# Reading the state operands of a chunked attention readout from a copy that is ordered by chunks

## The chip, the cores and the metric

The kernel runs on one core of a Trainium2 chip. The metric is the device time of one execution in microseconds (us), median of several runs. TensorE (PE) multiplies matrices; a weight load (PEld) puts the stationary operand into the array, a matmul streams the moving operand past it. VectorE (DVE), ScalarE (ACT) and GpSimd (POOL) do the elementwise work, and SyncE (SP) issues most transfers.

## The reference

Three stages follow one another: a linear attention with a decay per key dimension, an MLP, and a mixture of experts with one expert per token.

```python
# attention: B=4, H=8, S=768, D=48
for t in range(S):
    state = alpha[:, :, t, :, None] * state + k[:, :, t, :, None] * v[:, :, t, None, :]
    y[:, :, t] = einsum('bhd,bhde->bhe', q[:, :, t], state)
# MLP over 3072 tokens of 384: h = x @ w_in (384x2048); x = (h - tanh(h)) @ w_out
# experts: e = argmax(x @ w_gate); out = gate * sigmoid * (relu(x @ w1[e]) @ w2[e])
```

## The kernel before

Tokens are worked off in 8 blocks of 384 (half a sequence of one batch entry). A **unit** is one block of one pair of heads, so a block has 4 units and there are 32. The two heads of a pair lie on partitions 0 to 47 and 64 to 111. Within a unit the 384 tokens are 6 chunks of 64.

For each unit: `prep_k` and `prep_q` scan the decays and scale keys and queries (DVE); `decay` writes the chunk decays into `GE` (ACT, L196); `turn_k` transposes the keys (PE, L226, copied out by ACT); `score` multiplies keys and queries within a chunk (PE, L242 and L243, stationary operand `kt`, 48 rows by 64 contiguous columns); `causal` masks the scores (DVE); `carry` and `update` put the state increments of the chunks into PSUM (L259, L268); `chain` runs one scan on DVE over them (L272) and writes the states ahead of every chunk to `SS[p]`, a tile of [128, 64, 7]: for each of 48 value dimensions (padded to 64) the 7 states stand next to each other, so that the 64 values of one chunk's state row are 7 elements apart. `readout` (L306) then adds, for each chunk, queries times state and scores times values: 12 matmuls with `SS` as the stationary operand and 12 with `WV`, whose 64 columns are contiguous, over the four 64x64 quarters of the array, into one PSUM pair. The trace shows each of these fp32 matmuls as two instruction pairs. ACT copies the result out (L309), `place` splits off its low part (DVE, L315) and SP moves it into the MLP's input `xT`.

The MLP of a block is 16 steps f: `h_step` (L409, 9 matmuls into `psh`, tanh on ACT L415, subtraction on DVE L419, cast to a high part on ACT L423, low part on DVE L424) and `x_step` (L434, 9 matmuls) of the step before. The units of the next block are woven into these steps, one unit per 4 steps: in phase 0 (f % 4) score, carry and update, in phase 1 chain, in phase 2 readout, in phase 3 turn_k.

Units 0 to 3 run ahead of block 0, in an order written out by hand. Units 4 to 7 run in block 0's steps (`first_block`), also in an order written by hand for PE, ACT, DVE and POOL, along with the conversion of the MLP's weights. From block 1 on the framework's scheduler orders PE, ACT, DVE and POOL by its own timeline model; SP's order is by hand until block 2. Units 8 to 31 run in blocks 1 to 6. Block 7 has no units, and the experts follow it (L936, L964, L870, L871, L982). Each engine takes its instructions in order.

Of the kernel before, what the change touches and what calls it, by code (L numbers as in the profile page):

```python
# [9 lines left out]
F32 = mybir.dt.float32  # L10
# [8 lines left out]
B, H, S, D = 4, 8, 768, 48  # L19
# [7 lines left out]
NC = TB // CH  # L27
NBLK = NT // TB
NP = H // 2
# [34 lines left out]
def tile_kernel(ctx, tc, aps, outs):  # L64
    nc = tc.nc
    pe, act, dve, pool, sp = nc.tensor, nc.scalar, nc.vector, nc.gpsimd, nc.sync
# [14 lines left out]
    ap1 = att.enter_context(tc.tile_pool(name="ap1", bufs=1, side="right"))  # L81
# [41 lines left out]
    X0 = [ap1.tile([128, TB], F32, name=f"X0{i}") for i in range(2)]  # L123
# [2 lines left out]
    WV = [ap1.tile([128, WW], F32, name=f"WV{i}") for i in range(2)]  # L126
    GE = [ap1.tile([128, D, NC + 1], F32, name=f"GE{i}") for i in range(2)]
    VZ = [ap1.tile([128, NA, 2, 2 * D], F32, name=f"VZ{i}") for i in range(2)]
    SS = [ap1.tile([128, 64, NC + 1], F32, name=f"SS{i}") for i in range(NP)]

    early = [(psx, "x0"), (psx, "x1"), (psx, "x2"), (psa, "at")] * 4
# [6 lines left out]
    def pair(name):  # L138
        return psy.tile([128, 2, 512], F32, tag="py", name=name)

    units = [(j, p) for j in range(NBLK) for p in range(NP)]
# [18 lines left out]
    def vz(u):  # L160
        return vzx[u] if u in vzx else VZ[u % 2]

# [89 lines left out]
    def carry(u):  # L252
# [5 lines left out]
        else:  # L258
            act.copy(pu[:, 0:n * D:n], SS[p][:, 0:D, NC])  # L259

# [10 lines left out]
    def chain(u):  # L271
        yield dve.tensor_tensor_scan(  # L272
            out=SS[units[u][1]][:, 0:D].rearrange("p d c -> p (d c)"), data0=GE[u % 2].rearrange("p d c -> p (d c)"),
            data1=st[u].pop("pu")[:, 0:(NC + 1) * D], initial=0.0, op0=ALU.mult, op1=ALU.add)

    def weave(*gens):
        gens = [iter(g) for g in gens]
        while gens:
            for g in list(gens):
                if next(g, gens) is gens:  # L280
                    gens.remove(g)
# [3 lines left out]
    def readout(u):  # L285
        j, p = units[u]
        s = st[u]
        ps = s.pop("py") if u >= NP else pair("psy")
        SP, h = SS[p], NC // 2

        for c in range(h):
            for x in range(2):
                for q in range(2):
                    for hh in range(2):
                        cc = q * h + c
                        cs = slice(cc * CH, (cc + 1) * CH)
                        o = ps[64 * q:64 * q + 64, hh, c * CH:(c + 1) * CH]
                        if x == 0:  # L300
                            rs = slice(64 * hh, 64 * hh + D)
                            w, m = SP[rs, :, cc], X0[u % 2][rs, cs]
                        else:
                            rs = slice(64 * hh, 64 * hh + CH)
                            w, m = WV[u % 2][rs, cc * D:cc * D + 64], X1[rs, cs]
                        pe.matmul(o, w, m, start=(c + x == 0), stop=(x == 1), skip_group_check=True)  # L306
        s["y"] = y = (g3.tile([128, 2, TB], F32R, tag="gg", name="y") if 0 < u < 4 else ap1.tile([128, 2, TB], F32R, tag="y", name="y"))
        s["py"] = ps
        act.copy(y[:, 0].rearrange("p (b t) -> p b t", b=2), ps[:, :, 0:TB // 2])  # L309
# [80 lines left out]
    def gate(f):  # L390
        wT, pl = gated.pop(f)
        for k in range(KC):
            pe.matmul(pl, wT[:, k], wg[:, k], start=(k == 0), stop=(k == KC - 1), skip_group_check=True)  # L393
        act.copy(WR[f][:, DM:DG], pl)

    def conv_next():
        nonlocal nconv
        nconv += 1
        return conv(nconv - 1)
# [75 lines left out]
    rs = {}  # L475
# [198 lines left out]
    for i in range(2):  # L674
        pool.memset(VZ[i][64:128, :, 0], 0.0)
        pool.memset(VZ[i][0:64, :, 1], 0.0)
        pool.memset(WV[i][:, NC * D:WW], 0.0)
    for p in range(NP):
        pool.memset(SS[p][:, D:64], 0.0)
    warm = psh.tile([128, 512], F32, tag="h", name="warm")  # L680
    junk = ones1[:, 0:192].bitcast(BF16)

# [13 lines left out]
    def K(u):  # L696
        weave(prep_k(u))
        turn_k(u)
# [63 lines left out]
    def first_block(f, pend):  # L762
        u, ph = NP + (f + 1) // 4, f % 4
        new = [conv_next()] if nconv < NF else []

        def head():

            gate(f)
            if ph == 0:
                if f:  # L770
                    decay(u)
                carry(u)
                score(u)
                update(u)
            elif ph == 1:
                if u > NP:
                    alpha_low(u)
            elif ph == 2:
                readout(u)
            act.copy(OH[:, f], WR[f])  # L780
            if f + 1 < NF:
                low_in(f + 1)
            for g in new:
                for _ in range(4 if wide else 0):
                    next(g)

        def middle():
            weave(*new)
            if pend and ph != 3:
                x_step(*pend)  # L790
            if ph == 0:
                weave(chain(u))
            elif ph == 1:
                weave(causal(u))
                weave(prep_k(u + 1))
            elif ph == 3:
                x_step(*pend)
                turn_k(u)
                weave(prep_q1(u))
                weave(prep_q2(u))  # L800

        gg = h_step(0, f, (head,))
        middle()
        if f >= NF - 2:
            low_out(f - NF + 2)
        if ph == 0:
            load_v(u + 2)
        elif ph == 1:
            if u > NP:
                load_unit(u + 2)  # L810
        elif ph == 2:
            place(u)
            load_w_v(u + 2)
        if f + 1 < NF:
            gate_turn(f + 1)
        if ph == 3:
            scale_k(u)
        if f == NF - 1:
            decay(u)
            alpha_low(u)  # L820
            load_unit(u + 2)
        return gg

    pend = None
    for j in range(NBLK):
# [163 lines left out]
        for f in range(NF):  # L989
            g = j * NF + f  # L990
            u, ph = 4 + (g + 1) // 4, g % 4
            live = u < len(units)
            if j == 0:
                pend = 0, f, first_block(f, pend)
                continue
            pre = []
            if ph == 1 and live:
                pre.append(chain(u))
                if u + 1 < len(units):
                    pre.append(prep_k(u + 1))  # L1000
            if ph == 2 and u + 1 < len(units):
                pre.append(prep_q(u + 1))
            weave(*pre)
            if j > 0 and f == 2:
                route_score(j - 1)
            if j == 1 and f + 2 < NF:
                low_out(f + 2)
            gg = h_step(j, f)
            if ph == 0 and live:
                score(u)  # L1010
                carry(u)
                update(u)
                if u + 2 < len(units):
                    load_v(u + 2)
                weave(causal(u))
            elif ph == 2 and live:
                readout(u)
                if u + 1 < len(units):
                    alpha_low(u + 1)
                if u + 3 < len(units):  # L1020
                    load_unit(u + 3)
                if u + 2 < len(units):
                    load_w_v(u + 2)
                place(u)
            elif ph == 3 and live:
                turn_k(u)
            if pend is not None:
                x_step(*pend)
                if pend[1] == NF - 1:
                    evac(pend[0])  # L1030
            if j == 1 and f < E:
                sp.dma_start(out=rows[f * NT:f * NT + CAPS[0]].rearrange("(n p) c -> p n c", p=128),
                             in_=blank.unsqueeze(1).to_broadcast([128, CAPS[0] // 128, ROW]))
            if j == 1 and f == 12:
                route_send(0)
            if j > 0 and 2 <= f <= (2 if j == 1 else 3):
                (route_rank, route_send)[f - 2](j - 1)
            pend = (j, f, gg)
            if last:
                if f == 4:  # L1040
                    order()
                    fetch(0, 0)
                    fetch(0, 1)
                if f == 5:
                    gather(0)
                if 8 <= f < 15:
                    split(0, f - 8)
                    if f < 13:
                        fetch(0, f - 6)
                if 10 <= f < 10 + KC:  # L1050
                    turn_x(0, f - 10)
# [156 lines left out]
```

## Time and profile before

| | |
|---|---|
| median of 3 runs | 833.27 us (831.03 to 833.64) |
| profiled execution | 833.43 us, span 831.6 us |
| mean granted TensorE clock | 0.985 of 2.4 GHz |
| busy: PE, DVE, ACT, POOL | 803.4, 476.7, 343.6, 131.5 us |

The span runs from the first to the last instruction of the profiled execution; the time of an execution also holds what lies around it. An engine that is busy for nearly the whole span bounds the kernel where its stream has no gap; idle time of another engine costs nothing by itself.

### The profile page before, as it was taken

How to read it: one execution, taken by the hardware profiler on the slowest of the kernel's cores; microseconds unless marked ns; L12 is line 12 of the kernel's file. 1: busy time of each engine (PE TensorE's matmuls, PEld its weight loads, DVE VectorE, ACT ScalarE, POOL GpSimd, SP SyncE). 2: the span in 40 equal slices, each digit the busy share in tenths (PEclk: the TensorE clock that was granted, in tenths of full speed). 3: DMA queues.
4: the chain of work that ended last, by engine and by line, in shares of the span. 5: the costliest groups of instructions: out<-in, count | busy, mean ns of one | idle time of the engine just before them, and what ended most of it. 6: DMA issues, size and time to landing. Idle time of an engine off the chain costs nothing.

```text
span 831.6 us, 16944 instructions
## 1 busy us (share of the span) xinstructions
PE 803.4 (97%) x6688; PEld 745.6 (90%) x6688; DVE 476.7 (57%) x1050; ACT 343.6 (41%) x767; POOL 131.5 (16%) x120
## 2 busy tenths in 40 slices
PE   6699999999999999999999999999999999999995
PEld 4477887999999999999999999999999999999995
DVE  6878888766656665656755753445543434444321
ACT  4445554334434333443433442345443434444421
POOL 1000000020200200200100020021332314424321
PEclk8799999999999999999999999999999999999998
DMA  8465634753323322322332220034525426325400
GB/s 274 145 219 201 209 96 129 241 184 95 97 67 92 95 66 75 111 66 70 88 103 60 71 66 16 15 124 127 176 95 192 151 72 220 136 81 199 158 26 30
DMA packets 64358, 98.53 MB, mean 118 GB/s; under 512 B 20235, under 2 KB 52768, under 8 KB 64272
## 3 DMA queue, kind: packets, MB, share of 16 engines
q1 hardware_dynamic: 60864, 87.91, 34.2%
q0 software_dynamic: 3408, 9.47, 3.0%
q8 instruction: 54, 0.88, 0.4%
q14 instruction: 32, 0.26, 0.1%
HBM read 72.13 MB, written 16.25 MB: 106 GB/s over the span
## 4 chain that ended last, share of the span: by engine, by line
PE 84%; issue 5%; DVE 4%; ACT 3%; DMA 2%; SPq 1%; POOL 1%; POOLq 0%; ACTq 0%; DVEq 0%
PE x L434 26%; PE psh L409 23%; PE o L964 11%; PE psf L936 11%; PE psy L306 4%; PE psu L268 2%; PE psy L242 2%; PE pst L226 1%; PE warm L685 1%; PE pst L915 1%; ACT kt L204 1%; DMA raw<-raw 1%; PE pso L393 1%; DMA s<-w 1%; POOL out L982 1%
## 5 line engine op out<-in xcount | busy, mean ns | idle before, releaser
L409 PE MATMUL psh<-xT,IH 128*128 128x384 f32 x768 | 204.0, 342 | 0.0
L434 PE MATMUL x<-OH,gg 128*128 128x400 f32 x672 | 186.0, 351 | 1.1 <-DVE gg L424 0.5
L409 PEld LDWEIGHTS psh<-xT,IH 128*128 128x128 f32 x768 | 138.3, 189 | 1.0
L409 PE MATMUL psh<-xT,IL 128*128 128x384 f32 x384 | 129.9, 338 | 0.0
L419 DVE TENSOR_TENSOR t<-psh,t 128x384 f32<-128x384 f32 x128 | 70.9, 554 | 97.4 <-ACT t L415 96.8
L434 PEld LDWEIGHTS x<-OH,gg 128*128 128x128 f32 x672 | 121.5, 188 | 5.4 <-DVE gg L424 1.1
L415 ACT ACTIVATE t<-psh 128x384 f32<-128x384 f32 x128 | 62.7, 490 | 130.0 <-PE psh L409 124.5
L434 PE MATMUL x<-OL,gg 128*128 128x400 f32 x336 | 115.9, 345 | 0.0
L964 PE MATMUL o<-hi,hh 128*128 128x384 f32 (+2 forms) x440 | 115.1, 338 | 0.0
L936 PE MATMUL psf<-xe,hi 128*128 128x256 f32 (+6 forms) x432 | 109.3, 338 | 0.0
L942 DVE SCALAR_TENSOR_TENSOR hh<-psf,hh 128x384 fp32r<-128x384 f32 (+3 forms) x96 | 40.9, 447 | 91.8 <-ACT hh L940 90.8
L424 DVE TENSOR_TENSOR gg<-t,gg 128x384 fp32r<-128x384 f32 x112 | 63.6, 568 | 50.1 <-ACT gg L423 47.7
L423 ACT CAST gg<-t 128x384 fp32r<-128x384 f32 x112 | 57.3, 512 | 57.3 <-DVE t L419 56.1
L964 PEld LDWEIGHTS o<-hi,hh 128*128 128x128 f32 (+2 forms) x440 | 78.2, 184 | 1.2 <-DVE hh L942 0.2
L936 PEld LDWEIGHTS psf<-xe,hi 128*128 128x128 f32 x432 | 75.7, 188 | 2.7 <-issue 0.3
L964 PE MATMUL o<-lo,hh 128*128 128x384 f32 (+1 forms) x232 | 77.7, 337 | 0.0
L940 ACT ACTIVATE hh<-psf 128x256 fp32r<-128x256 f32 (+6 forms) x72 | 34.9, 484 | 95.1 <-PE psf L936 75.2
L409 PEld LDWEIGHTS psh<-xT,IL 128*128 128x128 f32 x384 | 72.4, 188 | 0.8
L936 PE MATMUL psf<-xe,lo 128*128 128x256 f32 (+6 forms) x216 | 71.9, 333 | 0.0
L201 POOL TENSOR_TENSOR kt<-kh,rP 128x384 f32<-128x384 f32 x24 | 20.0, 835 | 289.8 <-PE psy L243 166.4
L871 POOL TENSOR_TENSOR lo<-s,hi 128x768 fp32r<-128x768 f32 (+1 forms) x24 | 48.9, 2038 | 94.7 <-ACT hi L870 94.3
L434 PEld LDWEIGHTS x<-OL,gg 128*128 128x128 f32 x336 | 63.2, 188 | 0.0
(146 smaller groups left out, 1151.8 us busy)
## 6 DMA issues: line engine op xcount, KB each, us to landing
raw<-raw SPq DMA_DIRECT2D x32, 579.5 KB
wst<-wio SPq DMA_DIRECT2D x16, 768.0 KB
s<-w SPq DMA_DIRECT2D x24, 512.0 KB
s<-w SPq DMA_DIRECT2D x32, 384.0 KB
xT<-y SPq DMA_DIRECT2D x96, 72.0 KB
rows<-blank SPq DMA_DIRECT2D x8, 772.0 KB
WV<-vw SPq DMA_DIRECT2D x32, 144.0 KB
VZ<-vn SPq DMA_DIRECT2D x60, 72.0 KB
```

Of the source, the lines that this page charges most:

```text
L306: pe.matmul(o, w, m, start=(c + x == 0), stop=(x == 1), skip_group_check=True)
L409: pe.matmul(begun[f][:, 0:TB], w[:, f, c], xT[j][:, x, kc], start=(kc + n == 0), stop=(kc == KC - 1 and n == 2))
L415: act.activation(out=t, in_=ps[:, 0:TB], func=AF.Tanh)
L419: dve.tensor_tensor(out=g, in0=ps[:, 0:TB], in1=t, op=ALU.subtract)
L423: act.copy(gg[:, 0], g)
L424: dve.tensor_tensor(out=gg[:, 1], in0=g, in1=gg[:, 0].bitcast(F32), op=ALU.subtract)
L434: pe.matmul(px[j][a][:, 0:DG], g, w, start=(f == 0 and n == 0), stop=(f == NF - 1 and n == len(parts) - 1))
L871: (dve, pool)[i % 2].tensor_tensor(out=lo, in0=t, in1=hi.bitcast(F32), op=ALU.subtract)
L936: pe.matmul(ps[:, 0:n], w[:, kc, fs], xe[:, x, kc], start=(i == 0), stop=(i == 3 * KC - 1))
L940: act.activation(out=hh[:, 0:n], in_=ps[:, 0:n], func=AF.Relu)
L942: dve.scalar_tensor_tensor(out=hh[:, o:o + c.stop - c.start], in0=ps[:, c], scalar=0.0, in1=hh[:, c].bitcast(F32), op0=ALU.max, op1=ALU.su ...
L964: pe.matmul(po[q][m][0:p.stop - p.start, 0:DM], hh[:, p], w[:, f], start=(f == 0 and i == 0), stop=(f == NFE - 1 and i == len(parts) - 1))
```

## The change

A new tile `SC` of [128, 6, 64] is added, ordered by chunk and then by value dimension; POOL clears its padding once. For each unit from number 4 on, ACT copies the 6 used states of every value dimension out of `SS[p]` into `SC` (`by_chunk`), and `readout` takes its state operands from `SC`. Units 0 to 3 read `SS` as before. In block 0 the copy is issued in phase 1, behind the cast to `OH`; from block 1 on in phase 1, behind the issue of chain.

```diff
+    SC = ap1.tile([128, NC, 64], F32, name="SC")
     SS = [ap1.tile([128, 64, NC + 1], F32, name=f"SS{i}") for i in range(NP)]
...
+    def by_chunk(u):
+        act.copy(SC[:, :, 0:D].rearrange("p c d -> p d c"), SS[units[u][1]][:, 0:D, 0:NC])
...
-                            w, m = SP[rs, :, cc], X0[u % 2][rs, cs]
+                            w, m = SP[rs, :, cc] if u < NP else SC[rs, cc], X0[u % 2][rs, cs]
...
+    pool.memset(SC[:, :, D:64], 0.0)
...
             act.copy(OH[:, f], WR[f])
+            if ph == 1:
+                by_chunk(u)
...
             weave(*pre)
+            if ph == 1 and live:
+                by_chunk(u)
```

## Rows read from the trace of the kernel before

**Rows 1.** The page, part 1: busy us (share of the span) and instructions.
```profile
PE 803.4 (97%) x6688; PEld 745.6 (90%) x6688; DVE 476.7 (57%) x1050; ACT 343.6 (41%) x767; POOL 131.5 (16%) x120
```

**Rows 2.** Busy time by stretch: length, PE, PEld, DVE, ACT, POOL, clock, DMA.
```profile
45.00:130.00 85.00, 82.98 (x720) 67.88 (x718) 69.75 (x144) 42.01 (x118) 0.46 (x2) 1.00 0.54 176
130.00:200.00 70.00, 68.92 (x652) 62.68 (x651) 51.42 (x120) 28.65 (x71) 8.01 (x11) 1.00 0.57 178
...
265.30:330.60 65.30, 65.30 (x644) 61.88 (x643) 40.68 (x92) 26.35 (x61) 6.93 (x7) 1.00 0.30 83
```

**Rows 3.** Groups by line and form, readout and score: busy us, mean ns, idle.
```profile
L306 PEld LDWEIGHTS psy<-X,SS 48*64 48x64 f32 x768 | 32.3, 202 | 7.8 <-issue 7.4 <-DVE gg L424 0.3
...
L306 PEld LDWEIGHTS psy<-X,WV 64*64 64x64 f32 x768 | 23.7, 149 | 0.4 <-issue 0.4
...
L242 PEld LDWEIGHTS psy<-X,kt 48*64 48x64 f32 x336 | 21.6, 134 | 6.3 <-issue 6.2
```

**Rows 4.** TensorE's timeline, one steady readout: start us, us, instructions merged.
```profile
225.71 0.46 PE L306 MATMUL psy<-X,SS 48*64 48x64 f32 x8
225.99 0.30 PE L306 MATMUL psy<-X,WV 64*64 64x64 f32 x8
226.11 0.42 PE L306 MATMUL psy<-X,SS 48*64 48x64 f32 x8
226.34 0.30 PE L306 MATMUL psy<-X,WV 64*64 64x64 f32 x8
226.46 0.42 PE L306 MATMUL psy<-X,SS 48*64 48x64 f32 x8
226.70 0.30 PE L306 MATMUL psy<-X,WV 64*64 64x64 f32 x8
226.93 0.63 PE L434 MATMUL x<-OH,gg 128*128 128x400 f32 x2
```

**Rows 5.** TensorE's timeline, two score matmuls of one quarter, one after the other.
```profile
204.50 0.22 PE L242 MATMUL psy<-X,kt 48*64 48x64 f32 x1
...
204.56 0.22 PE L242 MATMUL psy<-X,kt 48*64 48x64 f32 x1
```

**Rows 6.** Groups by line and form: the subtract on DVE; casts and the decay copy on ACT.
```profile
L424 DVE TENSOR_TENSOR gg<-t,gg 128x384 fp32r<-128x384 f32 x112 | 63.6, 568 | 50.1 <-ACT gg L423 47.7 <-issue 1.7 <-ACT raw L219 0.6
...
L870 ACT CAST hi<-s 128x768 fp32r<-128x768 f32 x32 | 26.8, 836 | 0.0
...
L870 ACT CAST hi<-s 128x1024 fp32r<-128x1024 f32 x24 | 25.1, 1044 | 4.5 <-DMA s<-w 4.4
...
L196 ACT ACTIVATE GE<-P 128x288 f32<-128x288 f32 x32 | 22.9, 717 | 22.4 <-DVE SS L272 21.6 <-DVE P L188 0.8
```

**Rows 7.** Timelines of ACT and DVE around the readout of rows 4.
```profile
222.26 0.85 DVE L272 TENSOR_TENSOR_SCAN SS<-GE,psu 128x336 f32<-128x336 f32 x1
...
223.39 0.71 ACT L196 ACTIVATE GE<-P 128x288 f32<-128x288 f32 x1
...
224.10 0.50 ACT L423 CAST gg<-t 128x384 fp32r<-128x384 f32 x1
225.82 0.49 ACT L415 ACTIVATE t<-psh 128x384 f32<-128x384 f32 x1 [1.22 <-PE psh L409]
```

**Rows 8.** ACT's timeline in block 0, between chain and readout of a unit.
```profile
99.56 0.48 ACT L387 COPY wT<-pso 128x384 f32<-128x384 f32 x1 [0.84 <-PE pso L385]
```

**Rows 9.** Timelines of ACT and TensorE at unit 8, the first one of block 1.
```profile
144.09 0.73 ACT L196 ACTIVATE GE<-P 128x288 f32<-128x288 f32 x1 [0.76 <-DVE SS L272]
...
144.75 0.46 PE L306 MATMUL psy<-X,SS 48*64 48x64 f32 x8
```

**Rows 10.** Chain that ended last (a transfer), and TensorE's timeline behind it.
```profile
161.43 7.19 DMA raw<-raw
...
172.99 0.45 PE L434 MATMUL x<-OH,gg 128*128 128x400 f32 x1 [0.46 <-DVE gg L424]
```

**Rows 11.** Groups by line and form on POOL: the clearing of SS's padding.
```profile
L679 POOL MEMSET SS<- 128x112 f32 x4 | 0.6, 181 | 0.0
```

## Prediction

> **What bounds the kernel now.** I read the page first, then the busy time by stretches, then the groups by line and form, then single readouts on TensorE's timeline, and last ACT's timeline around the same readouts. On the page TensorE is busy for 97% of the span, the next engine for 57% [rows 1]. The stretches say where [rows 2]: in the first block, where attention and weight conversion share the machine, PE is busy 82.98 of 85.00 us; in the stretch from 130 to 200 us 68.92 of 70.00; in a whole block of the steady part 65.30 of 65.30 us, at a granted clock of 1.00 (the 2.4 GHz level), with DVE at 40.68 and ACT at 26.35 us. So from 45 us to the end of attention a microsecond taken out of PE's stream is a microsecond of the span, unless the stream then waits for something else, and a microsecond added to ACT is free as long as it fits into ACT's idle time and delays nothing that PE waits for.
>
> What PE does in a readout is what this change touches. One readout is 48 instruction pairs (24 matmuls of the source, each of which the trace shows twice): three groups of 8 with state operands (SS), three of 8 with value operands (WV). They have the same 64 columns and the same number of moving columns. The weight load of a state operand takes 202 ns, that of a value operand 149 ns [rows 3]. That this is not the 48 rows against 64 shows the score matmul: also 48 rows by 64 columns, from a tile in which those 64 columns lie next to each other, 134 ns [rows 3]. The states lie 7 elements (28 bytes) apart. The extra 53 to 68 ns are as much again as 64 columns seem to cost: consecutive score matmuls on the same quarter of the array start 0.06 us apart [rows 5].
>
> The starts on PE's timeline turn that into throughput [rows 4]. The readout begins at 225.71 us; the groups begin at 225.71 (SS), 225.99 (WV), 226.11 (SS), 226.34 (WV), 226.46 (SS), 226.70 (WV), and the next full-array matmul at 226.93. An SS group therefore holds the stream for 0.28, 0.23 and 0.24 us, a WV group between two SS groups for 0.12 us: 8 pairs over four quarters of the array are two passes each, 0.06 us a pass for WV and 0.12 us for SS. The readout as a whole takes 1.22 us.
>
> **The change, part by part.**
>
> *State operands from SC (28 readouts).* SC holds a chunk's 64 columns next to each other, as WV and kt do. An SS group at WV's pace takes 0.12 us in place of 0.23 to 0.24: 0.115 us less for the second and third group. The first takes 0.28, of which some 0.045 is more than its followers take; I let that stay (the array changes from whole to quarters there) and take 0.12 off. Sum per readout 0.12 + 0.115 + 0.12 = 0.355 us: 1.22 becomes 0.865. Bounds: nothing is saved if the load time is not the cause (a rival below); at most 0.40 us, if the first group also falls to 0.12. 28 x 0.355 = 9.9 us, at most 28 x 0.40 = 11.2. The number of PE instructions does not change. The row behind all this is 202 against 134 ns for loads of the same 48x64 [rows 3]. The Trainium skill, page "TensorE: Matmul & The Clock Gate", section "LDWEIGHTS (loading the stationary operand)", gives a load time that goes by the number of columns alone; by that the change would take nothing from PE and the time would stay at 833.4 us. The trace disagrees, with those two numbers. Another page of the Trainium skill, "SBUF — State Buffer", section "Door 1: The DMA port swizzle", says that each access that moves to a new 16-byte line of SBUF pays; by that an fp32 every 28 bytes pays each time and the saving stands, on which the trace agrees.
>
> *The copy on ACT (28).* 128x288 from SBUF to SBUF, read nearly contiguous (6 of every 7), written 256 bytes apart. No such row exists. Lower bound, from the contiguous casts: 768 elements take 836 ns and 1024 take 1044, 0.81 ns an element, so 288 take 836 - 480 x 0.81 = 446 ns. Upper: the decay copy of the same 128x288, which reads 260 bytes apart, 717 ns [rows 6]; with both sides slow perhaps 0.9 us. I take 0.72, since a far step on one side is what that row has. 28 x 0.72 = 20 us more of ACT, 0.72 x 4 = 2.9 us in a 65.3 us block in which ACT is idle for 39.
>
> The copy is hidden if it ends before the readout and what stands behind it on ACT still comes in time. Steady unit [rows 7]: the scan that writes the states starts at 222.26 and takes 0.85 (ends 223.11); the decay copy, which waits for that same scan, runs at 223.39 and is over by about 224.2; the readout begins at 225.71 [rows 4]. A copy between 224.2 and 224.9 ends 0.8 us ahead of it. Behind it stand the cast of the next hidden tile (224.10) and the tanh of 225.82, ahead of which ACT was idle 1.22 us. The cast moves to 224.9 and ends at 225.4, the DVE subtract after it (0.57 us [rows 6]) at about 226.0; the x matmuls that follow the readout would start at 225.71 + 0.865 = 226.6. Price if that cover is gone: up to 0.72 us a unit.
>
> In the first block the order is written out by hand and the copy stands behind the OH cast, one step after the scan and one before the readout. There ACT waited 0.84 us for PE ahead of 99.56 [rows 8]; the copy fits into it, and nothing of the readout waits, since it is a step away.
>
> *Two units where not all comes through.* Unit 8 (counted from 0): the decay copy started at 144.09, released by the scan, and the readout at 144.75 [rows 9]. A copy of 0.72 us, first or second in that place, ends at 144.8 to 145.7: between 0.1 and 1.0 us of wait, unless PE's order puts other matmuls there, of which it has plenty. I charge 0.4. Unit 9: its readout lies between the issue of a raw load and PE's wait for the work on that load: the transfer takes 7.19 us from 161.43, and PE's wait at 172.99 is released by DVE behind it [rows 10]. The 0.36 us saved between them only lengthen that wait: lost.
>
> *The rest.* One POOL memset of 96 elements a partition, nearest row 181 ns for 112 [rows 11], under PE's warm-up matmuls, on an engine that is busy 16% [rows 1]: nothing; POOL's first later compute of a unit is not before the ninth unit. No DMA is added and nothing on SP's queue moves. The scan may overwrite SS[p] as soon as the copy has read it rather than after the readout: never late. The copy waits for the readout four steps earlier to release SC: long past.
>
> *The sum.* 9.9 - 0.4 - 0.4 = 9.1 us. The profiled execution took 833.4 us (span 831.6); that gives 824.3. The median of the runs shown is 833.3, so the same number stands for the median.
>
> **Rivals.**
>
> *The load time has nothing to do with how far apart the columns lie.* The savings vanish, ACT's 20 us stay hidden: 833.4 us. For it: SS also differs from WV in its rows and in being the first of an accumulation. Against it: the score matmul has those 48 rows, starts its accumulation too, and loads faster still [rows 3]. Chance 0.04. The first of the two pages of the Trainium skill named above, "TensorE: Matmul & The Clock Gate", would make this the outcome.
>
> *Part of the saving is eaten.* From the second block on the order on PE, ACT and DVE comes from a scheduler with its own timing, and 24 more ACT copies may shuffle it: a tanh or cast lands 0.1 to 0.25 us too late in most units, or the wait at 172.99 grows by a microsecond or two. 28 x 0.1 to 28 x 0.25: 3 to 7 us of the 9 lost, 827 to 831. For it: the first readout after a change of block has the tighter cover (unit 8). Against: ACT's idle time ahead of the tanh, 1.22 us [rows 7]. Chance 0.07.
>
> *Slower: the copy goes onto PE's path.* PE takes its instructions in order; if ACT reaches the copy late, behind a cast that itself waits for DVE, the readout stalls with all x and h matmuls behind it. Fully exposed, the copy costs 0.72 plus some 0.06 of hand-over against 0.355 saved: 28 x 0.425 = 11.9 us, 845 us. It decides from 0.355 us of exposed wait per unit on, half the copy. For it: the readout's wait moves from DVE to an in-order engine with more in its queue. Against: 2.6 us between the end of the scan and the readout in the steady part [rows 4, 7]. Chance 0.05.
>
> **How the numbers follow.** Forecast 824.3 with chance 0.84. Its own bounds: 11.2 saved with nothing lost gives 822.2; 0.3 a readout less 1.4 for units 8 and 9 gives 833.4 - 7.0 = 826.4. For the range I add about a microsecond below, since the three runs of before lie 2.6 us apart, and above I go into the partly eaten case: 821.0 to 828.5. A measurement of this kernel can tell about 0.3%, 2.5 us, from no change. Faster by more: 0.84 and most of the partly eaten case, 0.89. Within: the rest of that and the first rival, 0.06. Slower: 0.05.
>
> **What would show it.** Right: the weight loads with SC at 134 to 150 ns (672 of them, 96 left with SS); a steady readout that takes 0.85 to 0.88 us from its first matmul to the next full-array one; PE's busy time lower by about 9 us with its idle time between 130 and 580 us still near 2 us or below; a new ACT group of 28 copies of 128x288 near 0.72 us, with no PE wait on it over a few tenths. Wrong: SC loads still near 200 ns (first rival), PE waits that name the copy or a late cast or tanh (second and third), or a copy well over 0.9 us.

## The result, and the profile after

The changed kernel takes 825.36 us (824.9 to 826.07, 4 runs) against 832.49 us, a ratio of 0.9916 with a 95% interval of 0.9896 to 0.9936. Run again later beside other kernels it took 826.11 us against 832.66, ratio 0.9937 (0.9916 to 0.9959). It is faster by 0.6 to 0.8%. The profiled execution took 825.11 us with a span of 823.3, 8.3 us less than before.

Engines over the whole span, the page's part 1; beside [rows 1] PE is busy 10.8 us less and ACT 14 us more (the 28 copies sum to 20.0 us; the records of neighbouring ACT instructions overlap in part):

```profile
PE 792.6 (96%) x6688; PEld 735.1 (89%) x6688; DVE 474.0 (58%) x1050; ACT 357.7 (43%) x795; POOL 130.9 (16%) x121
```

The groups by line and form. L311 is the readout, L279 the copy:

```profile
L311 PEld LDWEIGHTS psy<-X,WV 64*64 64x64 f32 x768 | 22.6, 144 | 0.0
...
L279 ACT COPY SC<-SS 128x288 f32<-128x288 f32 x28 | 20.0, 713 | 43.9 <-DVE SS L274 43.9
...
L311 PEld LDWEIGHTS psy<-X,SC 48*64 48x64 f32 x672 | 17.7, 133 | 6.2 <-issue 5.5 <-ACT t L420 0.5
...
L311 PEld LDWEIGHTS psy<-X,SS 48*64 48x64 f32 x96 | 4.8, 211 | 1.9 <-issue 1.9
```

A state operand from SC loads in 133 ns, where [rows 3] had 202 from SS and 134 for the contiguous score operand. The copy takes 713 ns, 28 times, and all the idle time ahead of it is waiting for the scan.

One steady readout on TensorE's timeline (start us, us), to be laid beside [rows 4]:

```profile
224.60 0.34 PE L311 MATMUL psy<-X,SC 48*64 48x64 f32 x8
224.76 0.30 PE L311 MATMUL psy<-X,WV 64*64 64x64 f32 x8
224.88 0.30 PE L311 MATMUL psy<-X,SC 48*64 48x64 f32 x8
224.99 0.30 PE L311 MATMUL psy<-X,WV 64*64 64x64 f32 x8
225.11 0.30 PE L311 MATMUL psy<-X,SC 48*64 48x64 f32 x8
225.23 0.30 PE L311 MATMUL psy<-X,WV 64*64 64x64 f32 x8
225.45 0.45 PE L439 MATMUL x<-OL,gg 128*128 128x400 f32 x1
```

Groups of state operands now hold the stream for 0.16, 0.11 and 0.12 us in place of 0.28, 0.23 and 0.24; the readout takes 0.85 us in place of 1.22. Of 28 x 0.36 = 10 us, 8.3 arrived between the two profiles, 0.7 of it ahead of readout 4, where TensorE does the same as before; by the medians it is 7.1. Where the rest went shows when the starts of the readouts on PE's timeline cut the span into stages (all in us; the last column is what 0.36 per readout in the stage would give):

| stage | before | after | difference | at 0.36 a readout |
|---|---|---|---|---|
| start to readout 4 | 57.55 | 56.86 | -0.69 | 0 |
| readout 4 to 8 (block 0, order by hand) | 87.20 | 85.77 | -1.43 | -1.44 |
| readout 8 to 14 (block 1 and into block 2) | 97.77 | 98.21 | +0.44 | -2.16 |
| readout 14 to 31 (blocks 2 to 6) | 276.88 | 271.14 | -5.74 | -6.12 |
| readout 31 to the end | 312.2 | 311.3 | -0.9 | -0.36 |

Block 0 gives exactly the sum, the steady part nearly, and the stage from readout 8 to 14 is 2.6 us short of it. (The first stage varies from 56.4 to 58.5 us among the profiles of kernels that are alike there.) Not all of the 2.6 is loss, because the stages do not hold the same work: on PE's timeline the changed kernel has 4 more x matmuls than the kernel before between readouts 8 and 14, 3 more between 14 and 31, and 7 fewer behind readout 31, each 0.18 us from start to start. With that taken out, the three stages are 1.9 us short, 0.2 us over and 0.7 us short. TensorE's waits from 130 to 580 us, in total, times, longest:

```profile
PE psh L414 <- DMA xT<-y: 0.9, 1, 0.9
PE psh L414 <- DVE t L424: 0.8, 1, 0.8
PE psy L244 <- ACT ktok L230: 0.7, 1, 0.7
PE psh L414 <- issue: 0.7, 1, 0.7
PE x L439 <- DVE lz L476: 0.4, 1, 0.4
```

None names the copy. The second is the wait behind the raw load of [rows 10]; the first and third are new and stand at the change from block 1 to block 2. The fourth is new too, at 518.4 us, at the start of block 7; the profile names no releaser for it, but the last piece of `xT` of the unit before landed at 518.2. The busy times by stretch (length, PE, PEld, DVE, ACT, POOL, clock, DMA), beside [rows 2], have the first and third in the second row:

```profile
130.00:200.00 70.00, 68.36 (x659) 62.91 (x657) 50.99 (x123) 31.53 (x77) 8.04 (x11) 1.00 0.57 175
200.00:265.30 65.30, 64.20 (x642) 60.64 (x643) 40.00 (x85) 28.45 (x68) 6.54 (x7) 1.00 0.31 87
265.30:330.60 65.30, 65.30 (x660) 61.63 (x660) 41.09 (x99) 29.66 (x69) 6.41 (x7) 1.00 0.32 90
```

The second stretch in the kernel before, where PE is busy throughout:

```profile
200.00:265.30 65.30, 65.30 (x644) 61.88 (x643) 40.59 (x90) 26.78 (x63) 6.92 (x7) 1.00 0.30 83
```

The chain that ended last, from the split of unit 11's result to block 2's first hidden matmul:

```profile
196.44 0.14 DVE y L320
...
197.71 0.64 SPq L330
...
198.40 0.59 SPq L330
...
199.03 2.23 DMA xT<-y
...
201.39 0.76 PE psh L414 x3
```

The unit's output leaves DVE, SP issues its pieces at some 0.6 us each, the last one lands 2.23 us later, and the next block's first matmuls stand in PE's queue and wait. TensorE's timeline there:

```profile
200.22 0.29 PE L244 MATMUL psy<-X,kt 48*64 48x64 f32 x2 [0.71 <-ACT ktok L230]
201.39 0.59 PE L414 MATMUL psh<-xT,IH 128*128 128x384 f32 x2 [0.88 <-DMA xT<-y]
201.82 0.33 PE L414 MATMUL psh<-xT,IL 128*128 128x384 f32 x1
202.08 0.27 PE L245 MATMUL psy<-X,kt 48*64 48x64 f32 x1
```

The score of unit 12 is broken in two, around the three waiting matmuls of the MLP. The kernel before does that score in one piece (0.85 us); here it takes 0.46 us more, the wait and the three matmuls not counted. The two new waits (1.6 us), this split (0.5) and the longer wait behind the raw load (0.3), less a gap of 0.26 us in unit 10's readout that the kernel before has and this one has not, come to 2.1 us, about the 1.9 that is missing.

### The profile page after: what moved, and what is told of

It reads as the page before. It is cut to its first block, busy times and chain, and to the rows that moved or that the text cites. A ratio compares the mean times of both kernels' runs of the same rounds, so it can differ in the third digit from the quotient of the medians.

```text
span 823.3 us, 16968 instructions
## 1 busy us (share of the span) xinstructions
PE 792.6 (96%) x6688; PEld 735.1 (89%) x6688; DVE 474.0 (58%) x1050; ACT 357.7 (43%) x795; POOL 130.9 (16%) x121
## 4 chain that ended last, share of the span: by engine, by line
PE 82%; issue 5%; DVE 4%; ACT 3%; DMA 2%; SPq 1%; POOL 1%; POOLq 0%; DVEq 0%; ACTq 0%
PE x L439 25%; PE psh L414 23%; PE o L972 11%; PE psf L944 11%; PE psy L311 3%; PE psu L270 2%; PE psy L244 2%; PE pst L228 1%; ACT kt L206 1%; PE pst L923 1%; DMA raw<-raw 1%; PE warm L691 1%; PE pso L398 1%; DMA s<-w 1%; POOL out L990 1%
```

## The experiments

The theory under test, called spacing theory in the expectations: the gain is the shorter load of contiguous columns, the copy is hidden, and what is missing sits in block 1. Rivals: the copy costs something, or the gain comes from the scheduler's other order of the work. All ratios are to the kernel before, measured beside each on the same chip. The kernel before took 832.5 to 833.5 us in the four sets of runs, so times of different sets are compared by their ratios.

**1. The copy alone.** The copy is made, the readout reads SS.

```diff
-                            w, m = SP[rs, :, cc] if u < NP else SC[rs, cc], X0[u % 2][rs, cs]
+                            w, m = SP[rs, :, cc], X0[u % 2][rs, cs]
```

> The copy to SC is made for units 4 to 31, but the readout takes its state operands from SS as before, so SC is never read. Spacing theory (the gain is the shorter weight load, the copy is hidden): SS loads stay at 202 ns and the time is that of before, 831 to 834 us. Copy rival (the copy itself costs one to two us somewhere): 834 to 836 us. Order rival (the gain comes from the scheduler putting the work in another order once the copy is in it): 825 to 828 us.

833.44 us against 833.45, ratio 0.9999 (0.9988 to 1.001). PE's instructions stand in the same order as before. The groups:

```profile
L311 PEld LDWEIGHTS psy<-X,SS 48*64 48x64 f32 x768 | 32.3, 202 | 7.7 <-issue 4.8 <-DVE gg L429 1.5 <-DVE r L486 1.3
...
L279 ACT COPY SC<-SS 128x288 f32<-128x288 f32 x28 | 20.0, 714 | 34.9 <-DVE SS L274 34.9
```

20 us of copies on ACT cost nothing, to within 1 us. The copy rival, which needs 1 to 2 us, falls. That the readout does not wait for the copy either is seen in the changed kernel, where no wait of PE names it.

**2. Block 0 alone.** Units 4 to 7, whose order is by hand, read SC; the others read SS and are not copied.

```diff
+                            w, m = SC[rs, cc] if NP <= u < 2 * NP else SP[rs, :, cc], X0[u % 2][rs, cs]
...
-            if ph == 1 and live:
-                by_chunk(u)
```

> Only units 4 to 7, whose order is written by hand, are copied and read from SC; units 8 to 31 read SS. Spacing theory: 4 x 0.36 to 4 x 0.40 = 1.4 to 1.6 us off, so 830.5 to 831.5 us, with readouts in block 0 some 0.39 us closer to one another than before (22.02 becomes 21.63). Order rival: the gain is all in the blocks that the scheduler orders, so 832 to 833 us and 22.0 us between the readouts of block 0.

831.66 us, ratio 0.9979 (0.9967 to 0.999). Readout 4 to 8 takes 85.69 us (before 87.20), from readout 14 to 31 276.89 (before 276.88). PE's order is that of before in every instruction, so here the gain cannot come from order: 1.5 us for four readouts. The order rival falls for these four; for the units that the scheduler orders run 5 decides.

**3. No copy.** SC is cleared once and never filled; the states are left out of the result.

```diff
     def by_chunk(u):
-        act.copy(SC[:, :, 0:D].rearrange("p c d -> p d c"), SS[units[u][1]][:, 0:D, 0:NC])
+        pass
...
-    pool.memset(SC[:, :, D:64], 0.0)
+    pool.memset(SC, 0.0)
```

> The readout takes its state operands from SC, but SC is only cleared once and never filled: the states are left out of the result and ACT has no copy. Spacing theory: SC loads 133 ns, 824.5 to 826.5 us, the same as with the copy. Copy rival: the copy's one to two us come back, 822 to 824 us. Order rival: without the copy the order is near that of before and little is gained, 830 us or more.

829.68 us, ratio 0.9955 (0.994 to 0.997): less work on ACT and, by the ratios, 1.5 to 3 us slower than with the copy. Spacing theory and copy rival both missed. The time lies at the edge of what the order rival expected (830 or more), but not for its reason: the loads are at 133 ns, and the order is neither that of before nor that of the changed kernel. In the steady blocks it breaks the first readout of a block in two; TensorE's timeline:

```profile
272.90 0.34 PE L311 MATMUL psy<-X,SC 48*64 48x64 f32 x6
273.17 0.64 PE L439 MATMUL x<-OH,gg 128*128 128x400 f32 x2
273.64 0.34 PE L439 MATMUL x<-OL,gg 128*128 128x400 f32 x1
273.91 0.27 PE L311 MATMUL psy<-X,SC 48*64 48x64 f32 x1
```

Six quarter-array matmuls, three of the MLP, and on with the readout: PE changes between the whole array and its quarters twice more. A block (readout 17 to 21) takes 64.29 us against 63.81 in the changed kernel and 65.28 before. So half a microsecond of a block's 1.47 hangs on order: the split readout with its three matmuls takes 0.45 us more than the two would in one piece each.

**4. The copy twice.**

```diff
+        act.copy(SC[:, :, 0:D].rearrange("p c d -> p d c"), SS[units[u][1]][:, 0:D, 0:NC])
         act.copy(SC[:, :, 0:D].rearrange("p c d -> p d c"), SS[units[u][1]][:, 0:D, 0:NC])
```

> Each unit's copy is made twice, one after the other, 28 more ACT instructions of 0.71 us (20 us of ACT in all). Spacing theory with a hidden copy: 825 to 827 us, since ACT has some 36 us of idle time in a 65 us block and the states are there 2.6 us ahead of the readout. Copy rival: the second copy costs what the first does, 827 to 829 us. If all of it lay on TensorE's path: 845 us.

832.42 us, ratio 0.9983 (0.9972 to 0.9994): a miss of all three. A steady block takes 64.66 us, yet PE does not wait in it:

```profile
265.30:330.60 65.30, 65.30 (x649) 61.29 (x648) 39.92 (x94) 30.67 (x70) 6.70 (x7) 1.00 0.30 83
```

ACT is busy 30.67 of 65.30 us. What changed is once more the order: the score of unit 20 is broken in two around three MLP matmuls, so that PE changes between the whole array, its halves and its quarters 22 times from readout 17 to 21, in place of 20. The split costs 0.44 us there, as in run 3, and one more MLP matmul (0.17 us) lies in the stretch; what makes the rest of the 0.85 us is not shown.

Two runs that alter ACT's load, one each way, both lose time by the order that they bring about, 1.5 to 3 us and 4 to 5.5 us by the ratios, so neither total prices a copy. Run 1, with the order unchanged, does, and so does block 0 of run 4: from readout 4 to 7, where PE's order is that of the changed kernel, the readouts follow one another at 21.63 to 21.64 us with two copies and at 21.61 to 21.65 with one.

**5. The distance between columns.** SC holds 2, 3, 4 or 6 chunks' elements side by side, so that the 64 columns of a chunk are 8, 12, 16 or 24 bytes apart (4 with one element left empty). PE's instructions stand in the same order as in the changed kernel. For 2:

```diff
-    SC = ap1.tile([128, NC, 64], F32, name="SC")
+    SC = ap1.tile([128, 3, 64, 2], F32, name="SC")
...
-        act.copy(SC[:, :, 0:D].rearrange("p c d -> p d c"), SS[units[u][1]][:, 0:D, 0:NC])
+        act.copy(SC[:, :, 0:D, 0:2].rearrange("p g d i -> p d g i"), SS[units[u][1]][:, 0:D, 0:NC].rearrange("p d (g i) -> p d g i", i=2))
...
-                            w, m = SP[rs, :, cc] if u < NP else SC[rs, cc], X0[u % 2][rs, cs]
+                            w, m = SP[rs, :, cc] if u < NP else SC[rs, cc // 2, :, cc % 2], X0[u % 2][rs, cs]
```

> SC holds two chunks side by side, so that a chunk's 64 columns are 2 elements (8 bytes) apart; copied on ACT as before. If the load slows with any gap: loads between 133 and 202 ns, about 150 to 170, and a readout of 0.95 to 1.1 us, 828 to 831 us. If it is the number of new 16-byte lines, with two columns in each: 133 ns, readout 0.86 us, 825 to 827 us.

> Three chunks side by side, columns 3 elements (12 bytes) apart: three of four columns open a new 16-byte line. By lines: loads between those of 2 and 4 elements apart, 150 to 202 ns, readout 0.95 to 1.2 us, 828 to 833 us. If only the gap as such counts: like the others with a gap.

> Columns 4 elements (16 bytes) apart, each one in a line of its own. By lines: loads at 202 ns as with 28 bytes, readout 1.22 us, no gain, 832 to 835 us. If the load grows with the bytes passed over: 160 to 185 ns and 828 to 831 us.

> SC in the order of SS without its seventh state: columns 6 elements (24 bytes) apart, the copy reads and writes nearly contiguously. Loads 202 ns, readout 1.22 us, 832 to 835 us. The copy tells what its far step cost: about 0.45 us if the 256 bytes between its writes made it 0.71, still 0.71 if the reading side or something else did.

Load and copy of each, by line and form; 8 bytes apart:

```profile
L311 PEld LDWEIGHTS psy<-X,SC 48*64 48x64 f32 x672 | 18.1, 136 | 6.1 <-issue 4.4 <-ACT t L420 1.6
L279 ACT COPY SC<-SS 128x288 f32<-128x288 f32 x28 | 12.8, 458 | 43.9 <-DVE SS L274 43.9
```

12 bytes apart:

```profile
L311 PEld LDWEIGHTS psy<-X,SC 48*64 48x64 f32 x672 | 23.0, 168 | 6.1 <-issue 4.4 <-ACT t L420 1.6
L279 ACT COPY SC<-SS 128x288 f32<-128x288 f32 x28 | 13.9, 495 | 43.9 <-DVE SS L274 43.9
```

16 bytes apart:

```profile
L311 PEld LDWEIGHTS psy<-X,SC 48*64 48x64 f32 x672 | 27.7, 202 | 6.2 <-issue 4.4 <-ACT t L420 1.6
...
L279 ACT COPY SC<-SS 128x288 f32<-128x288 f32 x28 | 12.2, 436 | 44.0 <-DVE SS L274 44.0
```

24 bytes apart:

```profile
L311 PEld LDWEIGHTS psy<-X,SC 48*64 48x64 f32 x672 | 26.8, 197 | 6.1 <-issue 4.4 <-ACT t L420 1.6
L279 ACT COPY SC<-SS 128x288 f32<-128x288 f32 x28 | 12.1, 433 | 43.9 <-DVE SS L274 43.9
```

| bytes between columns | load ns | readout us | time us | ratio (95%) |
|---|---|---|---|---|
| 4 (the change, run 7) | 133 | 0.86 | 826.11 | 0.9937 (0.9916 to 0.9959) |
| 8 | 136 | 0.87 | 829.1 | 0.9948 (0.9932 to 0.9964) |
| 12 | 168 | 1.05 | 833.44 | 1.0005 (0.999 to 1.0019) |
| 16 | 202 | 1.22 | 837.3 | 1.0051 (1.003 to 1.0072) |
| 24 | 197 | 1.19 | 836.14 | 1.0044 (1.0023 to 1.0065) |
| 28 (before) | 202 | 1.22 | | 1 |

Two columns in 16 bytes load as fast as four, one in 16 bytes takes half as long again, and more distance adds nothing. That is what the Trainium skill's page "SBUF — State Buffer", section "Door 1: The DMA port swizzle", gives with its 16-byte lines and two hits per line; these runs agree, with 136, 168 and 202 ns at 8, 12 and 16 bytes. Where the same passage goes on to give 4 fp32 as how far one can stride for free, they do not agree: that is the 16 bytes with 202 ns. The same page's rule shows on ACT's writes: 713 ns where each element goes 256 bytes from the last, 433 to 495 where two or more stay together.

The order is the same in all five kernels and the load alone differs: readout 14 to 31 takes 277.47 us at 16 bytes and 271.14 at 4, 0.37 us for each of the 17 readouts. So the order rival falls for the scheduler's units as well. With loads of 202 ns, copy and new order in place, the kernel is 0.5% slower than before; that is put down to the new order, since run 1 gives the copy no price. With 8 bytes the profile lost 1.6 to 2.2 us more between readouts 8 and 14 (100.39 us) than the two of the changed kernel, though PE's order is the same; in the readouts of units 10 and 12 it stood 0.4 us each for a reason that the profile doesn't name:

```profile
212.38 0.21 PE L311 MATMUL psy<-X,WV 64*64 64x64 f32 x1 [0.41 <-issue]
```

Before had such a gap too, in unit 10 (0.26 us). What it is stays open.

**6. Block 1 left as it was.** Units 8 to 11 read SS and are not copied.

```diff
+                            w, m = SP[rs, :, cc] if u < NP or 2 * NP <= u < 3 * NP else SC[rs, cc], X0[u % 2][rs, cs]
...
+            if ph == 1 and live and u >= 3 * NP:
+                by_chunk(u)
```

> Units 4 to 7 and 12 to 31 are copied and read from SC, units 8 to 11 (block 1) read SS, so that TensorE's order stays that of before up to unit 12. Spacing theory with the loss of some 2.8 us sitting in block 1's new order: 24 x 0.357 = 8.6 us off and no loss, 824 to 825.5 us, equal to or up to 1 us better than the changed kernel although four units gain nothing, and 80.9 us from readout 8 to readout 13 as before. If the loss belongs to the copy or to the faster stream as such: 8.6 less 2 to 3, 827 us.

825.31 us, ratio 0.9912 (0.9899 to 0.9925). Readout 8 to 14 takes 97.57 us: two readouts there gain, which would give 97.05. The 0.5 us above that are not lost either: the stage holds the same 4 x matmuls more (0.7 us) as in the changed kernel. From 14 to 31 it takes 271.15, as the changed kernel. TensorE's waits from 130 to 215 us no longer hold xT or ktok:

```profile
PE x L439 <- DVE gg L429: 0.8, 1, 0.8
PE x L439 <- DVE lz L476: 0.4, 1, 0.4
```

The loss between readouts 8 and 14 sits in block 1's new order: with that order avoided, four readouts that gain nothing are made up for. It is the order and not the faster stream that makes the two waits: in run 5's kernel with 16 bytes, new order and loads of 202 ns, they are there as well:

```profile
PE psh L414 <- DMA xT<-y: 0.8, 1, 0.8
PE psy L244 <- ACT ktok L230: 0.7, 1, 0.7
```

**7. The changed kernel again.**

> The changed kernel once more, as the measure beside the three others. 824.5 to 826.5 us, ratio to before 0.990 to 0.993. If block 1 is a matter of chance from execution to execution, its profile may show other waits between units 8 and 13 than the first did.

826.11 us, ratio 0.9937 (0.9916 to 0.9959), single runs from 825.25 to 830.32. Readout 8 to 14 takes 98.77 us, with the same waits on xT (0.9) and ktok (0.7), and 1.2 us in place of 0.8 behind the raw load. So the loss there, the 4 x matmuls taken out, is 1.9 to 2.4 us and comes back in each profile. Run 6, measured beside it, is 0.8 us faster; the intervals overlap.

**8. The first four units too**, in the changed kernel and in run 6. The edit in the changed kernel; in run 6's kernel block 1 goes on reading SS:

```diff
-                            w, m = SP[rs, :, cc] if u < NP else SC[rs, cc], X0[u % 2][rs, cs]
+                            w, m = SC[rs, cc], X0[u % 2][rs, cs]
...
         weave(chain(u))
+        by_chunk(u)
```

> Units 0 to 3 are copied and read from SC too. TensorE is busy 30.6 of the first 45 us there, so it is not the bound: the four readouts give back 0 to 1.4 us, and the copies, on an ACT that the chain of these units runs through, cost 0 to 2.9. Spacing theory: 824.5 to 828 us, no clear gain over the changed kernel. If the gain of a readout came through wherever it stands: 824 us.

> Both of these edits: every unit but those of block 1 reads SC. 823.5 to 827 us; the better of the two single edits tells which.

827.28 us (0.9935, 0.9922 to 0.9948) and 826.29 us (0.9914, 0.9899 to 0.9929), each about 1 us above its counterpart without the edit by the medians, with intervals that overlap: no gain, and no loss that is clear. Readout 4 starts at 59.62 and 59.48 us, 2 to 3 us later than in runs 7 and 6 (56.39, 57.63). There three copies stand on the chain that ended last (start us, us; of the first kernel):

```profile
13.13 0.69 ACT SC L279
...
20.98 0.57 ACT SC L279
...
29.07 0.60 ACT SC L279
```

The same copy that is free under a busy TensorE stands on the chain, 1.9 us for three, where the units run one after another.

## Why the prediction was right, point by point

The forecast was 824.3 us in a range of 821.0 to 828.5; measured were 825.4 and 826.1. The saving was forecast at 9.1 us; by the medians it is 7.1 and 6.6, between the profiles 8.3. That the time came nearer than the saving is in part luck: the forecast counted from 833.4, and the kernel before has a median of 832.5 with its fourth run.

- **The load.** Forecast 134 to 150 ns and 0.865 us a readout; measured 133 ns and 0.85 to 0.86. The first group fell from 0.28 to 0.16, as taken. Run 5 shows the reason, distance and nothing else, and the rule by which only the number of columns counts (the Trainium skill, "TensorE: Matmul & The Clock Gate", "LDWEIGHTS (loading the stationary operand)") does not hold here: 133 to 202 ns at the same 48x64.
- **The copy.** Forecast 0.72 us by the decay copy's row; measured 0.713, and no wait of PE on it. Run 1 shows that its work on ACT is free. Run 5 shows that the far writes were what made it slow. The row that the figure came from has its far step in the reads; that both cost the same was a guess that came true.
- **The places where not all comes through.** This term was mis-sized: 0.8 us forecast, 2.6 to 3.1 measured, 1.9 to 2.4 between readouts 8 and 14 and 0.7 behind readout 31. Unit 8 was to wait for its copy; no PE wait names it. Unit 9's saving did go into the wait behind the raw load: 0.75 us, where the same order with loads of 202 ns (16 bytes) has 0.47. What I did not see is the next wait in line, at the change of block, where the unit's output must pass SP and a transfer of 2.2 us before the next block begins, and where the scheduler had put that block's first matmuls ahead of other work: 1.6 us of new waits, and a score broken in two for 0.5. The 0.7 us stand at the change to block 7; that it is the same wait is inferred from the landing of the transfer.
- **PE's idle time.** I expected it near 2 us or below from 130 to 580 us; it was 3.5, mainly for the same reason. PE's busy time fell by 10.8 us, not 9.
- **The rivals.** That part of the saving is eaten by a changed order was given 0.07 as a case of its own. It happened in small, within the forecast's range. Runs 3 and 4 show how near the larger form was: orders that the same scheduler made for nearly the same program cost 1.5 to 5.5 us more.

## What to carry to other kernels

If TensorE bounds a stage, look at the weight loads of its small matmuls: columns of fp32 that are 16 bytes or more apart cost half as much again per load here (202 against 133 ns) and twice the stream time of a group (0.24 against 0.12 us), and a copy on an idle engine that puts them together, or two to 16 bytes, was free where its operands were there well ahead of the reader (2.6 us in the steady part). The same copy stands on the chain with its full length where the stages run one after another.

Where a scheduler writes the order, an edit changes the order too, and that can take back most of what the edit gives (run 4 has a ratio of 0.9983 in place of 0.992 to 0.994): price an edit in a part whose order stays (run 1, run 2), and cut the span into stages by an event that every version has before explaining a total. Then count the instructions of each stage: another order moves work across the cuts.

## What the runs showed of the hardware

The load time of a stationary operand went 133, 136, 168, 202, 197, 202 ns at 4, 8, 12, 16, 24 and 28 bytes between columns: free up to two columns in 16 bytes, and no worse beyond one. ACT's writes behave alike: 713 ns for 128x288 with single elements 256 bytes apart, 436 ns with three together.
